# Placing no-operations of TensorE by a list: some among the warm-up matmuls, the rest spread thinly ahead of the long runs of small matmuls

## The chip, the cores and the metric

The kernel runs on one core of a Trainium2 chip. The metric is the device time in microseconds of one execution. The kernel as it was took 286.43 us, the median of three executions at 285.24, 286.43 and 286.62 us. The profiled execution, from which every duration below comes, took 285.26 us.

## What is computed

A retention layer (attention with a fixed decay instead of a softmax) feeds a feed-forward layer with a squared ReLU. There are 8 batches, 8 heads, 576 positions and a head size of 64; the feed-forward layer works on 4608 tokens of width 512 with a hidden width of 2048.

```python
scores = scale * np.matmul(q, k.transpose(0, 1, 3, 2))
Dmat = np.where(rel >= 0, gamma[:, None, None] ** rel[None, :, :], 0.0)
x = np.matmul(scores * Dmat, v)          # heads side by side: 4608 x 512
h = x @ w_in                             # 4608 x 2048
out = np.maximum(h, 0.0) ** 2 @ w_out    # 4608 x 512
```

The inputs and the output are float32; the products are made from float16 copies.

## The kernel before

The 4608 tokens are cut into 36 units of 128, and two units make a group, 18 groups in all. For each group TensorE makes the masked scores (tile `psc`), the running sums of the recurrence (`psS`) and the retention output (`psO`) in small 64x64 matmuls, each on one quarter of the array. They are issued by `quad` (line 499). Then come the two large products of the feed-forward layer: `ph` (line 1226, and 1069 in the three groups that use Strassen's scheme for it too) and `po` (line 1324, Strassen's scheme with seven quarter-size products, each cut into four tasks of two matmuls; line 1267 for the first group). VectorE, ScalarE and GpSimd cast the inputs, apply masks and decay, empty the accumulators and square.

The order of all work is fixed when the program is built. `Schedule.emit` runs a list scheduler over tasks, each with an engine, a modelled duration `dur`, a modelled start and a number `size` of TensorE instructions; the keys come from the table `PLACES`. TensorE therefore gets one static stream of instructions. In that stream each matmul is a pair, a weight load and the matmul itself: 4490 pairs, and 9436 instructions with the no-operations, waits and drains.

The stream contains two kinds of passage that matter here.

**The warm-up.** 34 matmuls of 128x512 on zeros (line 408, tile `warm`, task key 10**6, `size` 2) are spread over the first 17 us, ahead of and between the first real work. In the stream the order at the start is: 12 warm-up matmuls; 8 transposes of the first k (`psT`, line 581, waiting for VectorE's casts `kx`, line 566); 3 warm-up matmuls; 8 transposes of the first q (waiting for VectorE's casts `qx`, line 564); 6 warm-up matmuls; then the first scores and sums (`psc`, `psS`, line 499). The scores wait for the copies of the transposes out of the accumulators (`kqT`, line 598, three on ScalarE and one on VectorE), the sums for the casts `vx` (line 559), one of which is GpSimd's. After that the first groups go on in the same way, with single warm-up matmuls between.

**The long runs.** From the sixth group on, the small matmuls of a group stand in one run of 193 to 258 instructions (`f0` in `add_ret`): output of the older state, scores and sums of the next group, one ordering no-operation (line 940), then the rest of the output. There are 13 such runs. One more of 129 instructions belongs to the last group, and 12 shorter runs (64 to 129 instructions) to the first groups.

TensorE's instructions lie in memory and are fetched in blocks. `place_runs` pads the stream with no-operations (`self.filler`, line 393, an instruction that only TensorE's sequencer handles) so that the long runs come to lie at chosen places modulo 256 instructions. Before the change it does so by a rule: a run that is about to start outside a range of places is moved to a fixed one, and the padding is divided evenly, by number, over the tasks of at most 20 instructions since the last bigger one.

## Time and profile before

| what | before |
|---|---|
| median of three executions | 286.43 us (285.24, 286.43, 286.62) |
| the profiled execution | 285.26 us, of it 283.5 us from the first to the last instruction |
| TensorE busy with matmuls | 276.7 us of 283.5 us |
| granted clock of TensorE | full from 4.16 us on, half before |
| matmul 128x256, start to start | 109 ns |
| warm-up matmul 128x512, start to start | 427 ns at half clock, 216 ns at full clock |
| padding no-operations | 417 (136, 121, 84 and 76, ahead of the 1st, 5th, 7th and 9th long run), all between 61.6 and 184.5 us |
| long runs, from the last matmul before to the first after | 1.39 to 1.58 us for 226 or 258 instructions, 1.21 and 1.26 us for 193 |

Times in the profile are microseconds from the first instruction. A matmul's row is counted as busy time of TensorE (PE), its weight load as that of PEld; "PEldq" is the sequencer that hands both out. A no-operation is the sequencer's alone, and no engine is busy with it. Where a row of waits names "issue", the engine waited for nothing that the profile shows: it waited for its own sequencer.

### The profile page before, as it was taken

To read this page: it belongs to the slowest core of one execution; us is meant where nothing else is said; L and a number is where in the kernel's file an instruction comes from. 1 tells how busy PE (TensorE), PEld (TensorE's weight loads), DVE (VectorE), ACT (ScalarE), POOL (GpSimd) and SP (SyncE) were. 2 spreads that over 40 slices of the span, in tenths; PEclk is the share of its full clock that TensorE was granted. 3 is DMA by queue.
4 is the path that set the end of the run, shared out by engine and by line. 5 is a ranking of instruction groups with operands and counts; after the bars stand their busy time and mean duration, and the time that the engine had idled before them with its cause. 6 is when DMAs were issued, how large, how long until landed. Compare 5 with 4: busy or idle time off the path is not lost.

```text
span 283.5 us, 10916 instructions
## 1 busy us (share of the span) xinstructions
PE 276.7 (98%) x4490; PEld 236.3 (83%) x4490; DVE 194.7 (69%) x371; ACT 190.6 (67%) x360; POOL 86.4 (30%) x123
## 2 busy tenths in 40 slices
PE   7899999999999999999999999999999999999994
PEld 2578767887888888888888888888888999899884
DVE  3793489757676849735849496966887899765742
ACT  5559984678585858666676766577657486668830
POOL 6550036334324254333243433343333500000000
PEclk9999999999999999999999999999999999999999
DMA  7999999999788987999999879897999832020205
GB/s 212 290 206 207 260 317 238 171 230 165 174 202 190 235 187 167 229 209 190 159 242 224 201 170 185 169 177 185 218 189 217 158 94 79 2 76 1 76 0 150
DMA packets 119152, 50.00 MB, mean 176 GB/s; under 512 B 94784, under 2 KB 113728, under 8 KB 119104
## 3 DMA queue, kind: packets, MB, share of 16 engines
q1 hardware_dynamic: 114560, 44.84, 72.5%
q0 software_dynamic: 4224, 4.19, 9.0%
q8 instruction: 37, 0.61, 0.9%
q10 hardware_dynamic: 320, 0.26, 0.4%
q14 instruction: 11, 0.09, 0.1%
HBM read 36.70 MB, written 9.44 MB: 163 GB/s over the span
## 4 chain that ended last, share of the span: by engine, by line
PE 95%; POOL 2%; issue 2%; DVE 0%; POOLq 0%
PE po L1324 37%; PE ph L1226 37%; PE ph L1069 7%; PE psO L499 5%; PE po L1267 2%; PE psc L499 2%; PE psS L499 2%; PE warm L408 1%; PE psT L581 1%; POOL mask L348 1%; POOL vx L559 0%; POOL w_in L475 0%; POOL mask_full L340 0%; POOL mask_tail L340 0%; DVE o L1347 0%
## 5 line engine op out<-in xcount | busy, mean ns | idle before, releaser
L1226 PE MATMUL ph<-xT,w_in 128*128 128x256 f16 x960 | 117.5, 273 | 0.0
L1226 PEld LDWEIGHTS <-w_in 128*128 128x128 f16 x960 | 93.0, 98 | 12.4 <-issue 0.6
L1234 ACT ACTIVATE rl<-ph 128x512 f16<-128x512 f32 x120 | 70.3, 590 | 42.2 <-PE ph L1226 41.5
L1244 ACT ACTIVATE gT<-rl 128x512 f16<-128x512 f16 x101 | 63.5, 630 | 2.7
L1324 PEld LDWEIGHTS <-gS 128*128 128x128 f16 x544 | 51.4, 98 | 6.7 <-issue 0.4
L1324 PE MATMUL po<-wT,gS 128*128 128x256 f16 x408 | 55.2, 273 | 0.0
L1324 PEld LDWEIGHTS <-gT 128*128 128x128 f16 x408 | 39.3, 98 | 5.2 <-issue 0.4
L1297 DVE TENSOR_TENSOR gS<-gT,gS 128x512 f16<-128x512 f16 (+1 forms) x51 | 30.6, 607 | 10.2 <-ACT gT L1244 9.6
L1324 PE MATMUL po<-w_out,gT 128*128 128x256 f16 x272 | 37.6, 273 | 0.0
L529 POOL TENSOR_TENSOR v<-loads,vdec_full 128x512 f16<-128x512 f32 x24 | 25.9, 1079 | 32.2 <-DMA loads<-in_v_dram 22.9
L1297 DVE TENSOR_TENSOR gS<-gT 128x1024 f16<-128x1024 f16 x34 | 26.0, 769 | 12.0 <-ACT gT L1244 9.2
L513 POOL CAST kq<-loads 128x512 f16<-128x512 f32 x32 | 22.4, 698 | 37.9 <-DMA loads<-in_k_dram 29.0
L1347 DVE TENSOR_TENSOR o<-po,u 128x256 f32<-128x256 f32 x33 | 13.9, 422 | 21.9 <-PE po L1324 14.6
L524 POOL CAST kq<-loads 128x512 f16<-128x512 f32 x24 | 16.9, 702 | 37.3 <-DMA loads<-in_q_dram 37.3
L1337 ACT COPY u<-po 128x256 f32<-128x256 f32 x34 | 12.4, 369 | 16.6 <-PE po L1324 16.4
L895 DVE TENSOR_TENSOR xT<-psO,gam_full 128x512 f16<-128x512 f32 x28 | 18.6, 685 | 5.0 <-PE psO L499 4.9
L1324 PE MATMUL po<-wT,gT 128*128 128x256 f16 x136 | 19.0, 273 | 0.0
L1324 PE MATMUL po<-w_out,gS 128*128 128x256 f16 x136 | 18.7, 273 | 0.0
L835 DVE TENSOR_TENSOR rT<-psc,mask_full 128x512 f16<-128x512 f32 x24 | 15.7, 682 | 0.8 <-PE psc L499 0.8
L1103 DVE CUSTOM_DVE_ANT_0 gT<-ph,loads 128x512 f16<-128x512 f32 x18 | 12.0, 686 | 4.0 <-PE ph L1069 3.5
L1246 DVE TENSOR_TENSOR gT<-rl 128x512 f16<-128x512 f16 x19 | 10.2, 541 | 6.5 <-ACT rl L1234 6.3
L608 DVE TENSOR_TENSOR R<-stmp,dec 128x512 f16<-128x512 f32 (+1 forms) x18 | 12.7, 703 | 0.4
(101 smaller groups left out, 307.2 us busy)
## 6 DMA issues: line engine op xcount, KB each, us to landing
out_dram<-o SPq DMA_DIRECT2D x32, 256.0 KB, 2.7
loads<-in_k_dram SPq DMA_DIRECT2D x24, 256.0 KB, 4.7
loads<-in_q_dram SPq DMA_DIRECT2D x96, 64.0 KB, 3.3
loads<-in_v_dram SPq DMA_DIRECT2D x24, 256.0 KB, 3.8
w_in<-in_moe_w_in_dram POOLq DMA_DIRECT2D x4, 512.0 KB, 8.6
w_out<-in_moe_w_out_dram POOLq DMA_DIRECT2D x4, 512.0 KB, 13.9
pair_c<-in_k_dram SPq DMA_DIRECT2D x2, 512.0 KB
pair_c<-in_q_dram SPq DMA_DIRECT2D x4, 256.0 KB, 6.1
```

Source lines behind the costliest of these rows:

```text
L499: t = nc.tensor.matmul(out_, lhsT=lhsT, rhs=rhs, start=start, stop=True, skip_group_check=True, tile_position=(64 * row, 64 * col))
L513: op(out=out_.rearrange("p (n b a d) -> p n b a d", n=2, b=2, a=2), in_=in_.rearrange("p (a n b) d -> p n b a d", n=2, a=2))
L524: nc.gpsimd.tensor_copy(out=tile_of["kq", u][:, 1].rearrange("p (t a d) -> p a t d", t=4, a=2), in_=tile_of["q32", u].rearrange("p (a t) d ...
L529: nc.gpsimd.tensor_tensor(out=t, in0=tile_of["v32", u], in1=vdec[kind].rearrange("p (h o) -> p h o", o=1).to_broadcast([P, H, D]), op=ALU. ...
L835: tile_of["masking", g] = nc.vector.tensor_tensor(out=tile_of["rT", g][:, :, a], in0=tile_of["psc", g][a].rearrange("p (s n i) -> p s n i" ...
L895: nc.vector.tensor_tensor(out=tile_of["x", g].rearrange("p n (s e i) -> p e (n s) i", s=n, e=2)[:, c], in0=y.rearrange("p (o t r) -> p o r ...
L1069: nc.tensor.matmul(out_[:, e], lhsT=left[:, m, fi * P:(fi + 1) * P], rhs=right()[:, m], start=fresh and e == 0 and m == 0, stop=m == HK - ...
L1226: nc.tensor.matmul(tile_of["ph", g, fb][:, j, :], lhsT=w_in16[:, m, fi * P:(fi + 1) * P], rhs=tile_of["x", g][:, m, :], start=(m == 0), st ...
L1234: nc.scalar.activation(out=t, in_=tile_of["ph", g, fb], func=ACTF.Relu)
L1244: nc.scalar.activation(out=t, in_=rl, func=ACTF.Square)
L1297: (nc.gpsimd if eng == "POOL" else nc.vector).tensor_tensor(out=tile_of["S", g][:, k, sl], in0=in0(sl), in1=in1(sl), op=op)
L1324: nc.tensor.matmul(tile_of["pb", g, bank], lhsT=left(i), rhs=right[:, i, :], start=(start and i == 0), stop=(i == HF - 1), skip_group_chec ...
```

## The change

The rule is gone. In its place stands a list `PADS` with the number of no-operations for each passage. The first number, 140, goes among the first 15 warm-up matmuls. Each further number belongs to one run of over 190 instructions, in order, and goes among the tasks of at most 8 instructions that the model starts after 24 us and that stand between the run before and this one (for the first run: all such tasks up to it). Both are divided in proportion to the tasks' modelled durations.

```diff
-    BLOCK, EDGE, AHEAD_OF, SAFE = 256, 194, 130, (60, 196)
+    WARM, PADS = 15, (140, 34, 22, 4, 4, 49, 48, 38, 38, 42, 0, 0, 0)

     def place_runs(self, tasks):
-        at = 3
+        def spread(n, among):
+            total = sum(x["dur"] for x in among)
+            until, done = 0.0, 0
+            for x in among:
+                until += x["dur"]
+                upto = int(n * until / total + 1e-6)
+                x["pad"] += upto - done
+                done = upto
+
+        pads = iter(self.PADS)
+        spread(next(pads), [t for t in tasks if t["key"] >= 10 ** 6 and t["size"] == 2][:self.WARM])
         between = []
         for t in tasks:
-            if t["size"] > 200:
-                phase = (at - self.EDGE) % self.BLOCK
-                if not self.SAFE[0] <= phase <= self.SAFE[1]:
-                    n = (self.AHEAD_OF - phase) % self.BLOCK
-                    for i, x in enumerate(between):
-                        x["pad"] += n * (i + 1) // len(between) - n * i // len(between)
-                    at += n
-            at += t["size"]
-            if t["size"] > 20:
+            if t["size"] > 190:
+                spread(next(pads, 0), between or [t])
                 between = []
-            else:
+            elif t["size"] <= 8 and t["key"] < 10 ** 6 and t["start"] > 24.0:
                 between.append(t)
```

Nothing else changes. The matmuls of TensorE and the instructions of all other engines keep their order. In the built program there are 419 padding no-operations instead of 417:

| passage | before | after |
|---|---|---|
| behind the 1st warm-up matmul | 0 | 31 |
| behind each of the 2nd to 15th | 0 | 7 or 8 (109 in all; the first 12 warm-up matmuls get 116 of the 140, the three between the two blocks of transposes 24) |
| up to the first long run | 136 (34 tasks with 4 each, from 61.6 us on) | 34 single ones, from the 24th us of the model on |
| ahead of the other runs, in order | 0, 0, 0, 121, 0, 84, 0, 76, 0, 0, 0, 0 | 22, 4, 4, 49, 48, 38, 38, 42, 0, 0, 0, 0 |
| most behind one task of the feed-forward products | 4 | 2, mostly 1 |

The first instructions of the 13 long runs stood at the places 69, 255, 25, 235, 69, 55, 69, 63, 69, 255, 113, 51, 137 (modulo 256) and now stand at 107, 59, 89, 47, 65, 99, 67, 99, 71, 1, 115, 53, 139. The 12 shorter runs of the first groups move on by 140 to 165 instructions.

## The prediction

> **What bounds the kernel now.** I read the page's busy times first, then the waits of TensorE, then the rows of its weight loads (which show when its sequencer hands work out), and last the no-operations alone.

> ```profile
> span 283.5 us, 10916 instructions
> PE 276.7 (98%) x4490; PEld 236.3 (83%) x4490; DVE 194.7 (69%) x371; ACT 190.6 (67%) x360; POOL 86.4 (30%) x123
> q8 instruction: 37, 0.61, 0.9%
> ```

> TensorE is busy 276.7 of 283.5 us, so an edit counts by what it adds to or takes from TensorE's stream. The third line is TensorE's code: 37 packets of 0.61 MB / 37 = 16.5 KB, and 9436 instructions / 37 = 255 in each. So code comes in blocks of 256.

> ```profile
> PE warm L408 <- DVE wT L289: 1.3, 1, 1.3
> PE psT L581 <- DVE qx L564: 0.5, 1, 0.5
> PE psc L499 <- DVE kqT L598: 0.5, 1, 0.5
> PE psS L499 <- POOL vx L559: 0.3, 1, 0.3
> ```

> These are all of TensorE's waits for other engines (us in total, times, longest), and all lie before 11.2 us. From the first sums on (`psS`, 11.13 us) it is never kept waiting. The order of work is fixed, so whatever delays that point delays the end by as much.

> ```profile
> PEld L1324 <- issue: 0.8, 4, 0.2
> PEld L1226 <- issue: 0.6, 3, 0.2
> 67.53 0.13 PEld L1324 LDWEIGHTS <-gS 128*128 128x128 f16 x2 [0.18 <-issue]
> 67.88 0.13 PEld L1324 LDWEIGHTS <-gS 128*128 128x128 f16 x2 [0.22 <-issue]
> L393 PEldq NOP  x417: 13/13/13, 61.6 to 184.5; - x139
> L393 PEldq NOP  x4: 13/13/13, 67.3 to 67.5; - x4
> ```

> Here the sequencer itself is late. The two timeline rows are neighbouring tasks of two matmuls with four no-operations ahead of each: they come 0.35 us apart, where two matmuls need 2 x 109 = 218 ns. The last row asks for the no-operations of 67.27 to 67.51 us. Each is shown as 13 ns long, but they start at 67.281, 67.352, 67.423 and 67.494 us: **71 ns apart**. That is the commonest distance of the 417 (none is below 70 ns; in twos it is often 90). A group of four and its two matmuls come every 303 ns at best, so the four other instructions cost (303 - 4 x 71) / 4 = 5 ns each. A no-operation thus takes the sequencer as long as 14 ordinary instructions. Mostly that is hidden: the no-operations are handed out up to 34 weight loads and matmuls (17 pairs, 1.9 us) ahead of the array.

> **The change, part by part.**

> *The dense no-operations go.* Taking each start-to-start time of matmuls that has four no-operations within it: 13 in `ph` have the usual 109 ns, 20 in `po` have 145 ns (16 of them) and 164 ns (4). With two or three between, all have 109 ns. So the old padding costs 16 x 36 + 4 x 55 = 0.8 us, all between 67 and 73 us. Afterwards at most two, mostly one, stand behind a task: 71 + 4 x 5 = 91 ns of the sequencer against 218 ns of matmuls. That is hidden. Term: **-0.8 us**.

> *140 no-operations among the warm-up.* Nothing like it is in the trace: all old ones stand after 61 us. Bounds: by their shown 13 ns, 140 cost 1.8 us of a sequencer that is idle there most of the time, so nothing; by their distance they take 140 x 71 = 9.9 us, and there is no lead behind which to hide them. The rows for the start:

> ```profile
> core 0: us, PE busy (x) PEld busy (x) DVE busy (x) ACT busy (x) POOL busy (x), PEclk, DMA share, GB/s
> 0.00:5.50 5.50, 4.18 (x12) 1.42 (x12) 2.16 (x32) 3.56 (x10) 4.11 (x22) 1.00 0.62 181
> 7.52 0.73 PE L581 MATMUL psT<-ident,qx 128*128 128x128 f16 x8 [0.48 <-DVE qx L564]
> 8.82 0.69 DVE L559 TENSOR_TENSOR vx<-pair_c,vdec_pair 128x512 f16<-128x512 f32 x1 [1.02 <-DMA pair_c<-in_v_dram]
> 9.43 0.68 DVE L598 COPY kqT<-psT 128x512 f16<-128x512 f16 x1
> 10.17 0.47 PEld L499 LDWEIGHTS <-kqT 64*64 64x64 f16 x30 [0.59 <-issue]
> 11.13 0.45 PE L499 MATMUL psS<-vx,kx 64*64 64x64 f16 x32 [0.32 <-POOL vx L559]
> ```

> The 12 warm-up matmuls ended by 5.5 us. I take the 71 ns. TensorE's sequencer is through its opening barrier at 0.79 us (the trace has that wait from 0.735 to 0.786 us). If it hands out no-operations while the first matmul still waits for `wT` (1.25 us), the transposes of q, which stand behind all 140 and 46 other instructions, come at 0.8 + 9.9 + 46 x 0.005 = 11.0 us instead of 7.52; if the wait holds it, at 11.4. I take 11.1. Then follow, as before, 8 transposes (0.45) and 6 warm-up matmuls (1.3): the scores start at 12.9. Their `kqT` copy no longer queues behind `vx` on VectorE (9.43) and is done at about 11.1 + 0.6 + 0.7 = 12.4, so it is not waited for. The scores take 0.55, and the sums, whose `vx` is long there, start at 13.4 instead of 11.13. Of the 3.6 us delay of the transposes, 1.3 us fall into waits that existed anyway. VectorE's masks of these scores were done 1.1 us before `psO` asked for them, so nothing further is late. Term: **+2.3 us**, bounds 0 and 2.7. The break-even is a no-operation of about 55 ns: then the transposes of q come at 8.8 us and the old waits swallow everything.

> *The clock.* The granted clock rose at 4.16 us, 2.9 us after the first matmul. With 8 no-operations (0.57 us) behind each 427 ns matmul the array idles a quarter of the time, and over half once matmuls take 216 ns. From 5.5 to 9.4 us it already idled in pieces of up to 0.5 us and kept the clock. Bounds: no loss, or another 2.9 us at half clock once real work has begun, 1.45 us. I take none; the pieces now are at most 0.36 us, but for one of 1.4 us behind the first matmul. [...]

> *The runs move.* A run is handed out as fast as the sequencer can, so what holds up the sequencer inside one shows. The old positions give 1.425 us (run of 258 starting at place 255), 1.441 (25), 1.563 (51), 1.527 (63), 1.425, 1.427 and 1.528 (all 69), 1.575 (113). Three runs at the same place differ by 0.1 us, so place explains at most 0.15 us. Those with place 194 in their last third have none of the extra gaps of 0.06 to 0.12 us that most others have a little behind it. Three runs (255, 25 and the 193-long one at 235) leave such favourable places for 59, 89 and 47; the other moved ones stay in the middle. Term: **+0.2 us**, bounds -0.4 and +0.8. What a run at a bad place would cost no row shows, as none stood there; neither does one now. [...]

> Sum on the profiled execution's own time: 285.26 - 0.8 + 2.3 + 0.2 = 286.96, so **287.0 us**. The profiled execution stands with the lowest of the three times (285.24); the median is 1.2 us above. Were the new kernel's median as far up, it would read 288.1.

> **The rivals.**

> *The warm-up hides its no-operations* (chance 0.30). For it: 71 ns is measured in a stretch full of other work, and 13 ns is what the row says; up to 55 ns cost nothing. Against: 70 is also the smallest distance there is. It gives 285.26 - 0.8 + 0.2 = 284.7, or 285.9 on the median's level.

> *A block of code that came late is no longer late* (0.10). Two of the three times lie 1.2 us above the other and the profiled one, as if something stalls in some executions. In the profile the first block's packet starts at 14.80 us and ends at 15.77; the short runs would want it at about 17. That margin of 1.4 us could fail in another execution. With 140 instructions ahead, block borders leave that spot. With the warm-up hidden as well, 284.0 to 284.7. Against: the profile shows no such stall, and a load that lands late would spread the times alike.

> *The thinned warm-up loses the clock* (0.15). [...] 285.26 - 0.8 + 2.3 + 0.2 + 1.45 = 288.4: slower than before. [...]

> **How the numbers follow.** The forecast has 0.45, with 286.6 to 288.1 as its own range. The range for all, 284.4 to 288.9, takes in the hidden warm-up on both levels, the late block's upper half and the lost clock on the lower level. A measurement of this kernel tells about 0.5% (1.4 us) from no change. Faster than 285.0 is the late block and a third of the hidden warm-up: 0.10 + 0.10 = 0.20. Slower than 287.9 is the lost clock and nearly half of the forecast (the upper level): 0.15 + 0.20 = 0.35. The remaining 0.45 is in between.

> **What would show it.** Right: no-operations about 71 ns apart from 0.8 to 11 us; the q transposes at about 11, the first sums at 13.4, with no waits on `kqT` and `vx`; weight loads of `po` without the 0.2 us gaps at 67 to 73 us. Wrong: the first sums still at about 11.1; a granted clock below full after 6 us; a gap over 0.3 us in a long run, which would make places matter more than I allow.

## The result and the profile after

| | before | after |
|---|---|---|
| median | 286.27 us (285.21 to 290.09, six executions) | 288.53 us (287.78 to 288.92, six) |
| ratio of times, 95% interval | 1 | 1.0088 (1.0063 to 1.0114) |
| profiled execution | 285.26 us | 288.64 us |
| its span | 283.5 us | 286.8 us |

The highest of the six times before, 290.09 us, is a slow execution and isn't in the ratio; the other five lie between 285.21 and 286.62 us, with a median of 286.12 us. The new kernel is slower by 0.9%, 2.3 us between the medians and 3.4 us between the two profiled executions. The page of the new kernel answers to the three lines shown of before:

```profile
span 286.8 us, 10918 instructions
PE 278.2 (97%) x4490; PEld 236.8 (83%) x4490; DVE 193.6 (67%) x371; ACT 190.4 (66%) x360; POOL 86.3 (30%) x123
q8 instruction: 37, 0.61, 0.9%
```

The work and the 37 packets of code are the same. The waits of TensorE (total, times, longest, in us) are:

```profile
PE warm L412 <- issue: 2.4, 4, 1.7
PE warm L412 <- DVE wT L293: 1.3, 1, 1.3
PE psS L503 <- issue: 0.3, 1, 0.3
PE psT L585 <- issue: 0.2, 1, 0.2
PE ph L1230 <- issue: 0.2, 1, 0.2
```

One row of its weight loads' waits has grown, that of the warm-up, shown before and after:

```profile
PEld L408 <- issue: 1.9, 7, 0.3
```

```profile
PEld L412 <- issue: 7.5, 12, 2.2
```

(Lines 408, 499, 581, 1226 and 1324 of before are 412, 503, 585, 1230 and 1328 here.) The recorded waits for `qx`, `kqT` and `vx` are gone, and so are the short gaps of line 1324. In their place stands the sequencer: the warm-up's weight loads wait 7.5 us for it instead of 1.9. The no-operations up to 11.8 us:

```profile
L397 PEldq NOP  x140: 13/13/13, 1.2 to 11.7; - x140
```

The 140 run from 1.246 to 11.75 us: with the pairs between them 75 ns for each. Most starts are 71 ns apart, but 24 of the 139 distances are 80 to 121 ns. The timeline of the start shows what follows behind them:

```profile
11.82 0.61 PE L585 MATMUL psT<-ident,qx 128*128 128x128 f16 x8 [0.24 <-issue]
12.46 0.58 ACT L602 COPY kqT<-psT 128x512 f16<-128x512 f16 x1 [0.78 <-PE psT L585]
13.08 0.69 DVE L602 COPY kqT<-psT 128x512 f16<-128x512 f16 x1 [2.92 <-ACT kqT L602]
13.65 0.81 PE L503 MATMUL psc<-kqT 64*64 64x128 f16 x32
14.25 0.46 PE L503 MATMUL psS<-vx,kx 64*64 64x64 f16 x32
```

The transposes of q come at 11.82 us instead of 7.52, the first sums at 14.25 instead of 11.13. Taking the whole TensorE stream of both profiled executions apart, start to start, gives:

| place | before | after | difference |
|---|---|---|---|
| first sums start | 11.13 | 14.25 | +3.12 |
| dense no-operations, 67 to 73 us | 0.78 | 0 | -0.78 |
| 13 long runs | 18.75 | 19.39 | +0.65 |
| gaps outside the runs that only after has | 0 | 0.42 | +0.42 |
| run of the first groups' sums | 0.77 | 0.70 | -0.07 |
| sum | | | +3.34 |

The last matmul starts 3.35 us later. Two of these terms are one kind of thing, a standstill of the whole stream. The first lies in plain feed-forward work, the second in the long run at 88.65 us:

```profile
183.00 0.60 PE L1230 MATMUL ph<-xT,w_in 128*128 128x256 f16 x4
183.80 0.60 PE L1230 MATMUL ph<-xT,w_in 128*128 128x256 f16 x4 [0.20 <-issue]
```

```profile
89.11 0.35 PE L503 MATMUL psS<-v,kq 64*64 64x64 f16 x19
89.77 0.31 PE L503 MATMUL psS<-v,kq 64*64 64x64 f16 x13 [0.32 <-issue]
```

Four matmuls of 109 ns should bring the next at 183.44; it comes 0.36 us late. In the run the gap is 513 ns where such gaps are about 60. Counted in the stream, the two late instructions have the places 194 and 195 modulo 256: the border of a block of code. The packets of the code queue tell when each block came. That of the first was fetched from 181.32 to 182.29 us, that of the second from 86.93 to 88.22, and each border was passed 1.5 us after the end of its packet.

### The profile page after: what moved, and what is told of

It reads as the page before. It is cut to its first block, busy times and chain, and to the rows that moved or that the text cites. A ratio compares the mean times of both kernels' runs of the same rounds, so it can differ in the third digit from the quotient of the medians.

```text
span 286.8 us, 10918 instructions
## 1 busy us (share of the span) xinstructions
PE 278.2 (97%) x4490; PEld 236.8 (83%) x4490; DVE 193.6 (67%) x371; ACT 190.4 (66%) x360; POOL 86.3 (30%) x123
## 4 chain that ended last, share of the span: by engine, by line
PE 97%; issue 1%; DVE 0%
PE ph L1230 37%; PE po L1328 37%; PE ph L1073 7%; PE psO L503 5%; PE warm L412 4%; PE po L1271 2%; PE psc L503 2%; PE psS L503 2%; PE psT L585 1%; DVE o L1351 0%; DVE wT L293 0%
## 5 line engine op out<-in xcount | busy, mean ns | idle before, releaser
L1230 PEld LDWEIGHTS <-w_in 128*128 128x128 f16 x960 | 93.2, 98 | 12.3 <-issue 0.4
L533 POOL TENSOR_TENSOR v<-loads,vdec_full 128x512 f16<-128x512 f32 x24 | 26.5, 1104 | 36.4 <-DMA loads<-in_v_dram 35.1
L1301 DVE TENSOR_TENSOR gS<-gT,gS 128x512 f16<-128x512 f16 (+1 forms) x51 | 29.1, 576 | 10.2 <-ACT gT L1248 9.5
L517 POOL CAST kq<-loads 128x512 f16<-128x512 f32 x32 | 20.9, 653 | 36.5 <-DMA loads<-in_k_dram 25.6
L528 POOL CAST kq<-loads 128x512 f16<-128x512 f32 x24 | 16.2, 675 | 34.0 <-DMA loads<-in_q_dram 33.8
L1341 ACT COPY u<-po 128x256 f32<-128x256 f32 x34 | 12.4, 368 | 16.5 <-PE po L1328 16.2
L412 PE MATMUL warm<-wT 128*128 128x512 f16 x34 | 12.6, 436 | 3.7 <-issue 2.4
L602 ACT COPY kqT<-psT 128x512 f16<-128x512 f16 x15 | 8.0, 591 | 10.4 <-PE psT L585 10.4
```

Of the source, the lines that this page charges most:

```text
L412: nc.tensor.matmul(warm_ps[0], lhsT=junk[:, 0:P], rhs=junk, start=True, stop=True)
L517: op(out=out_.rearrange("p (n b a d) -> p n b a d", n=2, b=2, a=2), in_=in_.rearrange("p (a n b) d -> p n b a d", n=2, a=2))
L528: nc.gpsimd.tensor_copy(out=tile_of["kq", u][:, 1].rearrange("p (t a d) -> p a t d", t=4, a=2), in_=tile_of["q32", u].rearrange("p (a t) d ...
L533: nc.gpsimd.tensor_tensor(out=t, in0=tile_of["v32", u], in1=vdec[kind].rearrange("p (h o) -> p h o", o=1).to_broadcast([P, H, D]), op=ALU. ...
L1230: nc.tensor.matmul(tile_of["ph", g, fb][:, j, :], lhsT=w_in16[:, m, fi * P:(fi + 1) * P], rhs=tile_of["x", g][:, m, :], start=(m == 0), st ...
L1301: (nc.gpsimd if eng == "POOL" else nc.vector).tensor_tensor(out=tile_of["S", g][:, k, sl], in0=in0(sl), in1=in1(sl), op=op)
```

## The experiments

The theory (1): the 140 no-operations hold TensorE's sequencer, 71 to 76 ns each, and delay the first sums; up to about 98 of them the waits that existed anyway hide them. The rivals: (2) the places of the runs cost, since a border that comes soon behind another finds its block not yet there; (3) the old kernel's times spread because its first code blocks are late in some executions, and the change only moves that. Each kernel is the new one with another list (the removed line is shown once). The comparisons stand against the kernel before on the same chip.

**The old places of the long runs, thin padding, nothing in the warm-up.**

```diff
-    WARM, PADS = 15, (140, 34, 22, 4, 4, 49, 48, 38, 38, 42, 0, 0, 0)
+    WARM, PADS = 15, (0, 136, 0, 0, 0, 121, 0, 84, 0, 76, 0, 0, 0, 0)
```

> No no-operations in the warm-up (0 instead of 140); the long runs at the places they had before the change, the 417 no-operations thinned as in the change. Theory 1 (the 140 hold up the start by 3.1 us, dense ones cost 0.8 us, places little): 0.8 us less than before on the profile's level, span 282.7, first sums (psS) at 11.1 us. Rival (the thin spreading or the new order of blocks costs, not the warm-up): about the time after the change, 2 us over before.

Measured: 285.41 us, ratio 0.9988 (0.9963 to 1.0013), span 283.7 us where 282.7 was expected. The dense gaps are gone (0.78 to 0 us), the long runs otherwise take what they took, but the fourth, at place 235, now takes 1.73 us instead of 1.26. The row is this one:

```profile
PE psc L503 <- DMA kqT<-kq: 0.4, 1, 0.4
```

From the sixth group on, the transposed k and q come by DMA, and in this run TensorE waits for them. Further the first sums came 0.34 us later (11.47 us) and their run in the first groups took 0.17 us longer: -0.78 + 0.47 + 0.34 + 0.17 = +0.20, the difference of the spans. In this profile the gain is there in its place and doesn't reach the end; the interval of the ratio would also allow the whole 0.8 us (0.9973).

**The new places, nothing in the warm-up.** The 140 go thinly ahead of the first long run.

```diff
+    WARM, PADS = 15, (0, 174, 22, 4, 4, 49, 48, 38, 38, 42, 0, 0, 0, 0)
```

> The changed kernel without the 140 in the warm-up; 140 more single ones between the 24th us and the first long run keep all long runs where the change puts them. Theory 1: 3.1 us less than after the change, so a span of 283.7 or less, and against the first experiment only what the places cost: 0.2 us of hold-ups in runs and between 0 and 0.9 us of late code blocks. Rival (the places make the loss): about as slow as after the change, 286.8.

Measured: 285.26 us, ratio 0.9991 (0.9971 to 1.0012). The long runs start where the changed kernel has them, and the loss is gone. So rival 2 doesn't carry the result: the places by themselves cost nothing that can be measured. In its profile, whose span is 284.0 us and not the expected 283.7 or less, the first sums start at 10.79 us, and the fourth long run waits again:

```profile
PE psc L503 <- DMA kqT<-kq: 1.2, 1, 1.2
```

**The old places, the 140 kept.**

```diff
+    WARM, PADS = 15, (140, 252, 0, 0, 0, 121, 0, 84, 0, 76, 0, 0, 0, 0)
```

> The 140 in the warm-up kept, the long runs at their old places (252 thin no-operations ahead of the first). Theory 1: the first sums at 14.25 us as after the change, 3.1 us over the first experiment, span 285.8, that is 0.8 to 1.0 us less than after the change. Rival (places): about the time of the first experiment.

Measured: 288.07 us, ratio 1.0079 (1.0049 to 1.0110), span 286.1 us where 285.8 was expected. The loss is back with the old places. The timeline of its start has the rows of the changed kernel to 0.01 us:

```profile
11.81 0.61 PE L585 MATMUL psT<-ident,qx 128*128 128x128 f16 x8
13.65 0.81 PE L503 MATMUL psc<-kqT 64*64 64x128 f16 x32
14.25 0.46 PE L503 MATMUL psS<-vx,kx 64*64 64x64 f16 x32
```

Its granted clock is full only from 11.07 us on, and the real work behind starts at the same time as with a clock that is full at 8.15. The late clock cost nothing here (first sums at 14.25 us in both), since the sequencer was the slower one: eight no-operations took it 0.6 us, a warm-up matmul at half clock 427 ns.

**90 and 115 in the warm-up** instead of 140; the rest goes ahead of the first long run, so all places behind stay.

```diff
+    WARM, PADS = 15, (90, 84, 22, 4, 4, 49, 48, 38, 38, 42, 0, 0, 0, 0)
```
```diff
+    WARM, PADS = 15, (115, 59, 22, 4, 4, 49, 48, 38, 38, 42, 0, 0, 0, 0)
```

> 90 no-operations in the warm-up instead of 140, the other 50 thin between the 24th us and the first long run; long runs as after the change. Theory 1 (75 ns each from 1.25 us on, and old waits that swallow the transposes of q up to 8.7 us, so about 98 are free): the transposes of q at 8.1 us, the first sums at 11.1 to 11.3, the time of the second experiment within 0.2 us. Rival (each one costs from the first, 22 ns on average as 3.1 us / 140): 2.0 us over the second experiment.

> 115 no-operations in the warm-up, the other 25 thin; long runs as after the change. Theory 1 (75.5 ns each from 1.25 us on, 98 free): transposes of q at 9.9 us, first sums at 12.3 us, that is 1.2 to 1.3 us behind the 90 of the fourth experiment and 1.9 us ahead of the 140. Rival (a jump at some place rather than a slope): first sums at 11.1 or at 14.25 us.

Measured: with 90, 285.60 us, ratio 0.9984 (0.9966 to 1.0003); with 115, one execution at 286.59 us. The start with 90, and then with 115:

```profile
8.13 0.61 PE L585 MATMUL psT<-ident,qx 128*128 128x128 f16 x8
9.96 0.81 PE L503 MATMUL psc<-kqT 64*64 64x128 f16 x32
10.99 0.45 PE L503 MATMUL psS<-vx,kx 64*64 64x64 f16 x32 [0.22 <-POOL vx L563]
```

```profile
9.96 0.61 PE L585 MATMUL psT<-ident,qx 128*128 128x128 f16 x8
11.79 0.81 PE L503 MATMUL psc<-kqT 64*64 64x128 f16 x32
12.39 0.46 PE L503 MATMUL psS<-vx,kx 64*64 64x64 f16 x32
```

The transposes of q come at 8.13, 9.96 and 11.82 us with 90, 115 and 140: 73 and 74 ns for each no-operation between. The sums, 10.99, 12.39 and 14.25 us, follow at the same slope from 115 on, while with 90 they still wait 0.22 us for GpSimd's `vx`, as before. That is a threshold and not a price: what is hidden doesn't delay the first sums, and each one beyond costs its 74 ns whole. The time with 90 is 0.3 us over the second experiment's, not within the expected 0.2; that is less than the two intervals can tell apart. Its profile has no wait in the fourth long run, but two standstills at borders between blocks of code, 0.56 and 0.20 us in small runs of the first groups, at 16.6 and 22.6 us.

**The runs moved on by 101 and by 145 instructions** against the old places. At the old places (the runs starting at 51 to 69) seven of the thirteen meet a border 125 to 143 instructions behind their start. With 101, these seven meet it after 24 to 42, just as they begin. With 145 they begin 2 to 20 instructions behind a border, and the longer ones meet the next near their end.

```diff
+    WARM, PADS = 15, (0, 237, 0, 0, 0, 121, 0, 84, 0, 76, 0, 0, 0, 0)
```
```diff
+    WARM, PADS = 15, (0, 25, 0, 0, 0, 121, 0, 84, 0, 76, 0, 0, 0, 0)
```

> The first experiment's kernel with 101 more thin no-operations ahead of the first long run, so that every long run starts 101 places later: seven of the thirteen have a border between code blocks (place 194) 24 to 42 instructions behind their start. Theory 2 (the next block is asked for when the border before it is passed, and can be used about 1.5 us after its packet's end, 4 to 6 us in all; such a run and the few matmuls behind it use up a block in 3 us): 1 to 3 us of standstill at the second border of each of the seven, 7 to 18 us over the first experiment. Rival (crossing a border costs at most the 0.1 us seen so far): within 1 us of the first experiment.

> The same with all long runs 145 places later than in the first experiment: four of them begin some 6 to 20 instructions behind a border and meet the next one near their end, three have a border 24 to 50 behind their start. Theory 2: the four have about 3.5 to 4 us between the two borders, as the sequencer passes the first one ahead of the array, so 0 to 2 us of standstill near the end of each, and 1 to 2 us at the three others: 2 to 14 us over the first experiment, less than with 101. Rival: within 1 us of the first experiment.

Measured: with 101, 287.64 us, ratio 1.0039 (1.0006 to 1.0071); with 145, 289.16 us, ratio 1.0108 (1.0068 to 1.0148). Both are slower than before, but the expectation was wrong: the 7 us and more of the first don't come, and the second is the worse. In the profiled execution with 101 the standstills are five of 0.06 to 0.41 us, 1.1 us in all; their packets began between 0.3 us before and 1.3 us after TensorE passed the border ahead. At 285.35 us it is the shortest of that kernel's executions, 2.3 us below its median, so what the others lost stands in no profile. With 145 the profiled execution is the longest of six (290.63 us). TensorE's waits and the worst of its long runs read:

```profile
PE psO L503 <- issue: 2.8, 4, 1.3
PE psS L503 <- issue: 1.4, 1, 1.4
...
PE ph L1230 <- issue: 0.6, 1, 0.6
```

```profile
163.57 0.29 PE L503 MATMUL psO<-rT,v 64*64 64x64 f16 x13
165.16 0.22 PE L503 MATMUL psO<-rT,v 64*64 64x64 f16 x3 [1.29 <-issue]
```

Of 16 equal matmuls, 13 run and three stand behind a border: the instruction at place 195 comes 1.49 us behind the matmul before it. All the other standstills of that kernel are at place 195 too (0.57, 0.82 and 0.73 us in long runs, 0.16 and 0.75 us in feed-forward work). The 1.4 us of `psS` fall into the first groups, at 19.3 us. Up to there the stream is the one of the kernel before, in whose three profiles the same place was late by 0.07 us at most; so they don't come from the move.

That standstills follow the borders is shown by the long runs, since only the padding was changed and the gap went to the new border. In the 13 profiles of this study 23 borders were passed late, by 0.06 to 1.5 us. How a block comes is read from the packets' times; what asks for it was not tried by itself. In the first 40 us a block's packet began 1.6 to 5.3 us after the array passed the border ahead, later on between 1.9 us before (the sequencer handed no-operations out up to 1.9 us ahead of the array in the profile of before) and 6.0 us after, with a median of 1.4 us after. The packets took 0.9 to 2.2 us. No border was passed sooner than 1.26 us after the end of its block's packet, and the 23 late ones were passed 1.26 to 1.68 us after it. So, in these profiles, a border was late when its packet was; those 23 lay 2.1 to 7.3 us behind the border ahead of them, while others lay only 2.0 us behind and were not late. In feed-forward work 256 instructions last 14 us (128 pairs of 109 ns), which leaves time for that. A long run passes them in 1.5 us, and a border shortly before it or shortly behind makes two that are close.

**The borders near the middle of eleven runs.**

```diff
+    WARM, PADS = 15, (0, 132, 57, 0, 33, 31, 15, 69, 25, 80, 80, 63, 84, 0, 0)
```

> No no-operations in the warm-up; 669 thin ones put the border near the middle (90 to 147 instructions in) of eleven of the thirteen long runs, which leaves the longest time to the borders before and behind. Theory 2: no standstill at a border; but as the old places show none either, the same time as the first experiment within 0.3 us; what remains are waits for the transposes by DMA at the fourth run. Rival (places still matter when all are safe): 0.5 us or more faster than the first experiment.

Measured: 286.46 us, ratio 1.0013 (0.9985 to 1.0042). No gain over the plain thin padding. None of the eleven runs has a standstill in its profiled execution. One of 0.93 us is in the run at place 25, one of the two others, whose border is 169 instructions in (its packet began 2.5 us after the border ahead was passed and took 1.2 us), and one of 0.8 us in the first groups' sums.

**The unchanged kernel twice more**, one profile each.

> The kernel before once more, for a second profile of the same program. Theory 3 (the first code block lands by chance before or after the sums of the second pair, `psS` at place 150, need it at about 17 us; in the first profile of before the run with that border took 765 ns, undisturbed ones 697): that run takes between 0.70 and 2.3 us, different from the first profile, and the time moves by as much. Rival (the spread of the times has another source): 0.70 to 0.77 us again, whatever the time.

> The kernel before a third time, for the same question: the run of `psS` with the first border in it takes between 0.70 and 2.3 us and explains most of the difference in time from the other two profiles (Theory 3), or 0.70 to 0.77 us whatever the time (rival).

Measured: 286.31 and 288.35 us. Rival 3 expected a late block among the first groups. The run of their sums took 0.70 and 0.72 us, no more than the 0.77 of the first profile, and so rival 3 falls as the cause of the spread of these three. (In the five other kernels with the same stream up to there it took 0.70 to 2.28 us, so such a block does come late in some executions.) What spreads is a wait in the fourth long run. In the longer of the two:

```profile
PE psc L499 <- DMA kqT<-kq: 2.7, 1, 2.7
```

```profile
115.82 0.30 PE L499 MATMUL psc<-kqT 64*64 64x64 f16 x16
118.77 0.32 PE L499 MATMUL psc<-kqT 64*64 64x64 f16 x16 [2.66 <-DMA kqT<-kq]
```

Half of the scores are through when the other half's operand is still on its way. The fourth long run took 1.26, 2.21 and 3.97 us in the three profiles of the unchanged kernel, at 285.26, 286.31 and 288.35 us. That is 0.95 and 2.71 us of differences of 1.05 and 3.09. In the same run the changed kernel and the one with the old places and the 140 took 1.16 us both: TensorE gets there 3 us later, and there is no wait.

**90 in the warm-up with the old places**, as a candidate for the best of both.

```diff
+    WARM, PADS = 15, (90, 46, 0, 0, 0, 121, 0, 84, 0, 76, 0, 0, 0, 0)
```

> 90 no-operations in the warm-up, 46 thin ones, the long runs at their old places: what the experiments so far would put together. Theories 1 and 2: first sums at 11.0 to 11.4 us, no standstill at a border in the long runs, a short one (0.3 to 0.8 us) at the second border near 16 us as in the fourth experiment, a wait for the transposes by DMA at the fourth long run: 0.2 to 0.8 us less than before. Rival (the early border decides): the same as before.

Measured: 286.09 us, ratio 1.0019 (0.9993 to 1.0044). The expected gain of 0.2 to 0.8 us didn't come. The profile has the wait in the fourth long run (0.8 us) and two standstills at borders in small runs of the first groups, 0.30 and 0.48 us. No kernel of this study is measurably faster than the one before.

## Why the prediction came out, point by point

**The dense no-operations, -0.8 us: right in place and size.** The sum was right, though not its parts: of the 20 starts in `po` that the prediction gives as 145 and 164 ns apart, ten have the usual 109 ns, three 122 to 157, five 195 and two 241 and 242 ns, again 0.8 us over the usual. The gaps of 0.78 us are gone in every kernel with thin padding. That they reach the end was assumed and isn't shown: the thin kernel is at 0.9988 (0.9963 to 1.0013). The prediction's "from the first sums on it is never kept waiting" holds for the one profile it was read from. In six of the ten other profiles without the 140 to hold it back, or with fewer, TensorE waited 0.4 to 2.7 us for the DMA's transposes in the fourth long run. The transfer decides more than TensorE's own time: in the kernel moved by 101 TensorE came to that run first of all, at 114.67 us, and waited under 0.3 us; in the unchanged kernel's third profile it came at 115.67 and waited 2.7.

**The 140 in the warm-up, +2.3 us: the right mechanism, sized too small; it is +3.12, beyond its upper bound of 2.7.** The prediction's two readings of the start were 0.8 us (the sequencer goes on while the first matmul waits for `wT`) and 1.25 us (it is held); the first no-operation starts at 1.246 us, so it is held. Times 75 ns instead of 71, the transposes come at 11.82 us, not 11.1, above the upper reading of 11.4 as well. About 0.1 us more comes from the `kqT` copy. The forecast had VectorE make it alone at 11.1 + 0.6; it comes behind ScalarE's last (12.46 to 13.04), runs from 13.08 to 13.77, and the second matmul of the scores starts 0.05 us after it ends. So the scores stretch from 13.65 to 14.25, 0.60 us instead of 0.55. The break-even was given as 55 ns for 140; it is now measured the other way round, as 98 no-operations at 74 ns (the sums with 115 come 12.39 - 11.13 = 1.26 us late, which is 17 of them; with 140 it is 3.12 us, which is 42; with 90 they come no later than before). These figures rest on the 11.13 us of one profile. In the unchanged kernel's other profiles the first sums start at 10.65 and 11.29 us, by which 91 to 100 are hidden; with the 140 they start at 14.25 us in both profiles.

**The clock, nothing: right, though a sign of being wrong came.** The prediction named a granted clock below full after 6 us as a sign of being wrong, and the clock was full at 8.15 us instead of 4.16, with an idle piece of 1.7 us behind the first matmul where 1.4 was expected. But that was before the work that counts, and even 11.07 us in another kernel cost nothing: its first sums start at 14.25 us, as in the changed one. The sign is no clear one either: in the eight profiles without no-operations in the warm-up the clock was full between 4.01 and 7.04 us. The rival of a lost clock falls: its 1.45 us, an estimate of the author's, shows in no run. In the changed kernel the clock, once full at 8.15 us, stayed full to the end of the span, over idle pieces of up to 0.24 us between the warm-up matmuls.

**The moved runs, +0.2 us: the size is inside the bounds, the reading behind it was wrong.** The long runs took 0.65 us more, of which 0.45 is one standstill, and outside them 0.42 us came that no term had. The remaining 0.2 us can't be told from chance: the twelve runs without the fourth took 17.49, 17.49 and 17.75 us in the three profiles of the unchanged kernel. Nor must the standstill in feed-forward work belong to the change, as the unchanged kernel's third profile has one of 0.34 us at the same border, at 184.21 us. The prediction named a gap of over 0.3 us in a long run as what would make places matter more than it allowed, and that gap came. A border cost more than the 0.12 us that the first profile showed, up to 1.5 us, where it was passed 1.26 to 1.68 us after the end of its block's packet. The first profile couldn't show it, since no packet was that late there. Most borders were not passed late in the 13 profiles, 23 of about 470 were; these lie in long runs, in the first groups and in feed-forward work.

**The sum.** On the profiled execution's own scale the forecast was 287.0 us and the profile gave 288.64: the error is 0.8 us at the start and 0.8 us of late blocks. On the medians it looked better: 288.53 against the 288.1 that the prediction gave for a median as far above as before. That closeness is partly luck. The profile of the unchanged kernel at 286.31 us, near its median, holds 0.95 us of waiting in the fourth long run, and the changed kernel, 3 us late there, no longer has it. That would explain why 3.4 us of loss between the profiles are 2.3 us between the medians. The changed kernel's times are also closer together, 1.1 us from end to end, where the unchanged kernel's (290.09 us left out) span 1.4 us here and 1.9 to 2.9 us in the larger sets beside the experiments. That the hold swallows this wait rests on two profiles with the 140, both without the wait, against those six with it; it wasn't tried by itself, and in the other profiles the late half of the scores started anywhere from 115.2 to 118.8 us, while the two reached it at 118.7 and 118.9.

**The rivals.** The hidden warm-up is refuted by the slope (74 ns each), though for the first 90 or so it holds. The late block exists (the first groups' sums took 0.70 to 2.28 us over the profiles of this study), but the changed kernel won 0.07 us by it.

## What to carry to other kernels

A no-operation whose row shows 13 ns is not free for that: here it held the sequencer 71 to 75 ns. Take the distance between starts, and ask at which count the waits that it may hide behind are used up: here about 98 delayed nothing, and each one beyond delayed the first sums by its whole 74 ns. If an edit makes a fully busy engine come sooner, look for what it will meet there: in one profile half of a gain of 0.8 us at 70 us was lost again at 116 us, waiting for a transfer. And take more than one profile of the kernel as it was before calling a difference of a few tenths of a per cent: three of one kernel differed by 3.1 us, 2.7 of it in a single wait.
